# Talking-heads attention and two MoE layers on one core: scores of two pairs of heads as one piece of work, with four score banks and two pre-mix banks

## The chip, the cores and the metric

The kernel runs on one core of one Trainium2 chip. The metric is the time of one execution on the device in microseconds; lower is better.

## What is computed

The reference, cut to what matters (12 heads, 4 batches, 448 rows, head size 64, all float32):

```python
scores = 0.125 * q @ k.T                            # per batch b, head h: 448 x 448
scores = einsum('bhij,hg->bgij', scores, w_pre)     # pre-mix over heads
attn = softmax(scores, axis=-1)
attn = einsum('bhij,hg->bgij', attn, w_post)        # post-mix over heads
x = (attn @ v) as 1792 tokens x 768
h = x @ w_in; x = (h * cos(h)) @ w_out              # 768 -> 2048 -> 768
logits = x @ phi                                    # soft MoE, 8 experts x 4 slots
slots = softmax(logits, axis=0).T @ x               # per expert: relu(slots @ w1[e]) @ w2[e]
out = softmax(logits, axis=1) @ slot_outputs
```

## The kernel before, in words

The kernel has three phases: attention (phase_a, to about 513 us of the profiled span), the first layer with the logits (phase_b) and the soft MoE (phase_c). Only phase_a is touched.

phase_a works through 16 tiles (line 216): four batches, each cut into three tiles of 120 query rows and one of 90. For each tile and each of six pairs of heads there is a score (lines 346 to 389). `mul` (353) multiplies q by k for the two heads of a pair. q and k are each split into a high and a low part, so there are three products; the two heads lie on the two halves of the partitions (64 rows each), and their matmuls stand in two row halves of the array, each head in a PSUM bank of its own. That makes six matmuls. `out` (361) copies each head's bank to SBUF on ScalarE or VectorE, into one of eight places (`ssrc`), and `sort` (372) issues a transfer on the SP or POOL queue that puts the head's rows into the tile's `s2` in the order that the pre-mix wants. `s2` has two places, one per tile.

A tile has four groups of 30 rows (three in the smallest tile), 60 groups in all. `pre` (394) does three pieces for each group: one pre-mix matmul by a 120 x 120 matrix over the whole array into a "pre" bank, then the maximum on VectorE (408) and the exponential on ScalarE (412); the bank is free after the exponential. It needs all twelve sorted heads of its tile. `fin` (422) makes the post-mix weights, `post` (436) does four pieces for each group, each of three products into a "post" bank that is copied out (448), and `av` (485) multiplies a tile's mixed attention by v in three pieces with matmuls of 64 columns (half the array), each into one bank of the kind "ps". `k_prep` (286) and `q_prep` (309) transpose k and q into "ps" banks, from where ScalarE and VectorE split them. Beside all that, `narrow` (505) converts the next phase's weights from 64 to 32 bits on ScalarE, VectorE and GpSimd.

PSUM has eight banks. Three are for the pre-mix ("pre"), two for the post-mix ("post"), three for scores, transposes and av ("ps"); `PLACES` (24) says so. For the first 24 pieces that ask for "ps", `SPARE` (26) takes banks of all three kinds in turn, since the others are not yet used.

The order of the work is not written out by hand: a planner (`Plan`, lines 72 to 176) makes it before the kernel is built. Every piece of work is an `op` with the engines that may do it and a price on each, the pieces that it depends on, the places that it takes or uses, and a due time in units of groups. `schedule` (114) goes forward in time: for each engine it looks at the pieces that can start within 0.05 us of the earliest (145), and takes the one that is due first. A piece can start when its engine is free, its inputs are done, and all the places that it takes are free (`room`, 96). TensorE's pieces that use half the array (scores and av, `half=True`) and those that use all of it have a price of `TURN` = 0.095 us for going from one to the other (134), and a piece that would change the mode counts as due `STAY` = 0.4 groups later (146). Each engine then runs its instructions in the planned order; the semaphores, not the plan's times, set when they start.

A score of pair p in a tile whose first group is g0 is due at g0 - 3.2 - 3.6 (5 - p) / 5 (568). `qk[ti, p]` is its matmul piece; the next tile's `q_prep` and the next batch's `k_prep` wait for it before they write over q and k (303, 338), and some loads are put behind it (566, 573).

Of the kernel before, what the change touches and what calls it, by code (L numbers as in the profile page):

```python
# [9 lines left out]
F32 = mybir.dt.float32  # L10
# [10 lines left out]
AHEAD_AT = [v for v in range(16, 48) if v % 2 == 0] + 2 * [48, 49, 50, 51] + [52, 55, 56, 58, 60, 61]  # L21
LATER = {4: [0], 8: [1], 11: [2], 13: [3], 14: [4]}

PLACES = {"pre": 3, "post": 2, "ps": 3, "knat": 2, "qnat": 2, "ssrc": 8, "s2": 2, "e": 3, "wc": 2, "xst": 1,
          "raw": 4, "nar": 5, "cv_t": 2, "cv_m": 2}
SPARE = 3 * ["ps", "pre", "ps", "pre", "ps", "post", "pre", "post"]

K_DUE, S_DUE, S_SPAN, P_DUE, AV_DUE, AV_SPAN, STAY = 4.0, 3.2, 3.6, 1.8, 0.7, 3.0, 0.4

# [149 lines left out]
def phase_a(tc, ident, q, k, v, w_pre, w_post, xT_d, wide, start_next):  # L179
    nc = tc.nc  # L180
    B, H, S, D = q.shape
# [6 lines left out]
    with ExitStack() as ctx:  # L188
        early = ctx.enter_context(ExitStack())

        sg = early.enter_context(tc.tile_pool(name="a_groups", bufs=1))
        sp = early.enter_context(tc.tile_pool(name="a_sb", bufs=1))
        sn = early.enter_context(tc.tile_pool(name="a_nar", bufs=1))
        sl = ctx.enter_context(tc.tile_pool(name="a_late", bufs=1, side="right"))
        pp = ctx.enter_context(tc.tile_pool(name="a_pre", bufs=PLACES["pre"], space=PSUM))
        pq = ctx.enter_context(tc.tile_pool(name="a_post", bufs=PLACES["post"], space=PSUM))
        ps = ctx.enter_context(tc.tile_pool(name="a_ps", bufs=PLACES["ps"], space=PSUM))

# [4 lines left out]
        def room(pool, tag, shape, dtype, name):  # L203
            return pool.tile(shape, dtype, tag=tag, name=name, bufs=PLACES[tag])

        kp = sp.tile([128, H // 2, S], F32R, name="k_hi")
        kr = sp.tile([128, H // 2, S], F32R, name="k_lo")
        vt = sl.tile([CJ, H, NJ, D], F32, name="v")  # L210
        qh = sp.tile([128, H // 2, 120], F32R, name="q_hi")
        ql = sp.tile([128, H // 2, 120], F32R, name="q_lo")
        am = [sl.tile([CJ, H, NJ, 120], F32, name=f"am{i}") for i in range(2)]
# [6 lines left out]
        QUEUE = {"SP": nc.sync, "ACT": nc.scalar, "POOL": nc.gpsimd}  # L220
        PSUMS = {"ps": ps, "pre": pp, "post": pq}
        plan = Plan(PLACES, SPARE)

        def copy(by, out, in_):
            if by == "DVE":
                nc.vector.tensor_copy(out=out, in_=in_)
            else:
                nc.scalar.copy(out=out, in_=in_)  # L228

        def bank(slot, name):  # L230
            return PSUMS[slot.tag_used].tile([128, 512], F32, tag=slot.tag_used, name=name)

        made = {}
# [5 lines left out]
        kload, qload, vload, knat, qnat = {}, {}, {}, {}, {}  # L239
# [16 lines left out]
        def load_q(ti, part, due, behind):  # L256
            b, t = tiles[ti]
            m = H // 3
            if part == 0:
                qslot[ti] = Slot("qnat")  # L260

            def start():
                if part == 0:
                    qnat[ti] = room(sp, "qnat", [120, H, D], F32, f"qnat{ti}")
                h = m * part
                for r, n, i in ((0, 80, 360), (80, 10, S - 10)) if t == 3 else ((0, 120, 120 * t),):
                    nc.sync.dma_start(
                        out=qnat[ti][r:r + n, h:h + m],
                        in_=q[b, h:h + m, i:i + n, :].rearrange("h i d -> i h d"))
            qload[ti, part] = dma(1.0 if t == 3 else 0.5, 0.65, start, due=due, late=3.0 if ti > 1 else 0.0, takes=[qslot[ti]] if part == 0 else [],  # L270
                                  uses=[] if part == 0 else [qslot[ti]],
                                  behind=behind + ([qload[ti, 0]] if part else []))

        def load_v(b, c, due, behind):
            def start():
                nc.sync.dma_start(
                    out=vt[:, 4 * c:4 * c + 4],
                    in_=v[b, 4 * c:4 * c + 4].rearrange("h (p t) d -> p h t d", t=NJ))
            vload[b, c] = dma(0.55, 1.9, start, due=due, late=5.0,
                              deps=[avs[4 * b - 1, c]] if b else [], behind=behind)  # L280


        kdone, qdone, qk, sdone, avs, amdone = {}, {}, {}, {}, {}, {}
        EV = [("ACT", 0.44), ("DVE", 0.56)]
# [58 lines left out]

        s2l, s2t, sorted_ = {}, {}, {}

        def scores(ti, p, due):

            b, t = tiles[ti]
            n = ROWS[t]
            s = [Slot("ps") for _ in range(2)]  # L350
            x = {}

            def mul(e):
                pts = made["s", ti, p] = [bank(s[o], f"s{ti}_{2 * p + o}") for o in range(2)]
                for i, (x, y) in enumerate(((qh, kp), (qh, kr), (ql, kp))):
                    for o in range(2):
                        r = slice(64 * o, 64 * o + 64)
                        nc.tensor.matmul(pts[o][:n, :S], x[r, p, :n], y[r, p, :],  # L358
                                         start=(i == 0), stop=(i == 2))

            def out(o):
                def f(e):
                    if ti:
                        x[o] = room(sg, "ssrc", [120, S], F32, f"ss{ti}_{2 * p + o}")
                    else:

                        c = S * (2 * p + o)
                        x[o] = am[1].rearrange("p h t i -> p (h t i)")[:, c:c + S]
                    copy(e, x[o][:n], made["s", ti, p][o][:n, :S])
                return f  # L370

            def sort(o):
                h = 2 * p + o

                def f(e):
                    if h == 0:
                        s2t[ti] = room(sg, "s2", [120, 12, S], F32, f"s2_{ti}")
                    QUEUE[e].dma_start(out=s2t[ti][h::12, :n // 10], in_=x[o][:n])  # L378
                return f
            qk[ti, p] = plan.op([("PE", 0.8)], mul, [kdone[b, p], qdone[ti, p // 2]], due, takes=s, half=True)  # L380
            for o in range(2):
                h = 2 * p + o
                ss = [Slot("ssrc")] if ti else []
                if h == 0:
                    s2l[ti] = Slot("s2")
                c = plan.op(EV, out(o), [qk[ti, p]], due, takes=ss, uses=[s[o]])
                sorted_[ti, h] = plan.op([("SP", 1.0), ("POOL", 0.8)], sort(o), [c], due,
                                         takes=[] if h else [s2l[ti]], uses=ss + ([s2l[ti]] if h else []),
                                         moves=1.0 * n / 120, behind=[sorted_[ti, 0]] if h else [])

# [3 lines left out]
        def pre(gi, c, due):  # L394
# [5 lines left out]
            def mul(e):  # L400
                if c == 0:
                    et[gi] = sl.tile([120, 3, S], F32, tag="e", name=f"e{gi}", bufs=PLACES["e"])
                    mz[gi] = sl.tile([120, 3, 3], F32, tag="mz", name=f"mz{gi}", bufs=PLACES["e"])
# [51 lines left out]
        xst, xl = {}, {}  # L455
# [107 lines left out]
        for b in range(B):  # L563
            for ti in range(4 * b, 4 * b + 4):
                g0, n = first[ti], NG[tiles[ti][1]]
                mark = [qk[ti - 1, 0]] if ti > 2 else [qk[1, 5]] if ti > 1 else [qk[0, 2]] if ti else []
                for p in range(6):
                    d = g0 - S_DUE - S_SPAN * (5 - p) / 5
                    if p % 2 == 0:
                        load_q(ti, p // 2, d - K_DUE - 2 if ti == 0 else d - 2.1, mark)  # L570
                    if ti % 4 == 0:
                        for t in range(NJ) if p % 3 == 0 else ():
                            load_k(b, p // 3, t, d - K_DUE - 2, [qk[4 * b - 2, 0]] if b else [])
                        k_prep(b, p, d - K_DUE)
                    if p % 2 == 0:
                        q_prep(ti, p // 2, d - 0.3)
                    scores(ti, p, d)
                for gi in range(g0, g0 + n):
                    for c in range(3):
                        pre(gi, c, gi - P_DUE + c / 3)  # L580
                    f = fin(gi, gi - 0.4)
                    for jt in range(NJ):
                        post(gi, jt, f, gi + jt / 4)
                if ti % 4 == 0:
                    for c in range(3):
                        load_v(b, c, g0 + 2, [] if b else [mixed[2]])
                if ti < NT - 1:
                    av(ti, g0 + n + AV_DUE)
        for u in range(len(units)):
            due = N_FIRST + (N_LAST - N_FIRST) * u / (len(units) - 1)  # L590
# [632 lines left out]
```

## Time and profile before

| | |
|---|---|
| median of 3 runs | 947.32 us (946.84 to 953.72) |
| the profiled execution | 947.2 us, its span 945.4 us |
| TensorE busy in the span | 901.4 us, 95% |
| VectorE, ScalarE, GpSimd busy | 70%, 60%, 21% |
| mean granted TensorE clock | 0.988 |

All stretches and single times below are in microseconds from the start of that span. The time is a little longer than the span, since it also has what lies around the first and last instruction. PE is TensorE, PEld its weight loads, DVE VectorE, ACT ScalarE, POOL GpSimd, SP the engine that issues most transfers; L358 is line 358 of the kernel. Matmuls are pipelined and their ends are modelled, so neighbouring PE rows overlap; the step from one start to the next tells what a piece takes. [...]

### The profile page before, as it was taken

What the parts mean: (1) busy time and instruction counts of PE and PEld (TensorE: products, weight loads), DVE (VectorE), ACT (ScalarE), POOL (GpSimd) and SP (SyncE); (2) the same over time, 40 slices, a digit from 0 to 9 for tenths busy, and PEclk for the clock granted to TensorE, in tenths of its full rate; (3) what the DMA queues carried; (4) which work ended last, traced back from release to release, by engine and by line L of the source; (5) the groups of instructions that cost most, each with busy time, mean ns of one, the idle gap of its engine ahead of it and who ended that gap; (6) DMA issues with size and microseconds to landing.
All of it is one profiled execution on the core that took longest, in us unless ns stands there. A gap on an engine that the chain in (4) does not pass through costs nothing.

```text
span 945.4 us, 18209 instructions
## 1 busy us (share of the span) xinstructions
PE 901.4 (95%) x6720; PEld 648.5 (69%) x6720; DVE 663.4 (70%) x1294; ACT 563.6 (60%) x1241; POOL 196.5 (21%) x242
## 2 busy tenths in 40 slices
PE   7889999999999999999999999999999999989985
PEld 4556767776777777676778877777777787945522
DVE  4658998988989889898844755666766667833303
ACT  4556786777777777777654654565657558610102
POOL 2032444524544336453400000000000000000000
PEclk9989999999999999999999999999999999999897
DMA  7999778898788978988338731364464339899999
GB/s 161 209 183 210 202 208 212 187 245 233 210 224 205 252 197 200 226 222 237 109 95 248 218 114 51 112 211 132 147 215 136 106 114 299 276 355 379 373 373 330
DMA packets 195460, 198.92 MB, mean 210 GB/s; under 512 B 70916, under 2 KB 164752, under 8 KB 195372
## 3 DMA queue, kind: packets, MB, share of 16 engines
q1 hardware_dynamic: 185176, 176.97, 64.3%
q0 software_dynamic: 7584, 20.14, 8.9%
q8 instruction: 53, 0.87, 0.4%
q10 hardware_dynamic: 2612, 0.65, 0.3%
q14 instruction: 35, 0.29, 0.1%
HBM read 135.40 MB, written 23.59 MB: 168 GB/s over the span
## 4 chain that ended last, share of the span: by engine, by line
PE 73%; DVE 12%; DMA 7%; ACT 3%; issue 3%; SPq 1%; DVEq 0%; ACTq 0%
PE po L443 11%; PE pre L405 10%; PE h L710 8%; PE h L711 8%; PE h L713 8%; PE av L467 5%; PE s L358 5%; PE gt L750 3%; DMA early<-in_moe_w_dram 3%; PE eh L1030 2%; DMA s<-ss 2%; DVE cvt L531 2%; DVE mz L408 2%; PE etr L1039 2%; PE lg L759 2%
## 5 line engine op out<-in xcount | busy, mean ns | idle before, releaser
L443 PEld LDWEIGHTS po<-wc,e 120*112 120x112 f32 x1440 | 171.8, 177 | 63.8 <-issue 41.7
L443 PE MATMUL po<-wc,e 120*112 120x120 f32 x1440 | 184.7, 270 | 2.3 <-ACT am L228 1.0
L405 PE MATMUL pre<-s,kron_pre 120*120 120x448 f32 x360 | 166.5, 550 | 5.2 <-ACT e L412 2.7
L710 PE MATMUL h<-x,wh 128*128 128x512 f32 (+1 forms) x384 | 142.0, 380 | 0.0
L412 ACT ACTIVATE e<-pre,mz 120x448 f32<-120x448 f32 x180 | 114.8, 638 | 44.0 <-DVE mz L408 41.4
L711 PE MATMUL h<-x,wh 128*128 128x512 f32 (+1 forms) x384 | 136.2, 364 | 0.0
L408 DVE TENSOR_REDUCE mz<-pre 120x1 f32<-120x448 f32 x180 | 110.4, 618 | 27.9 <-PE pre L405 26.8
L228 ACT COPY am<-po 112x360 f32<-112x360 f32 x184 | 84.6, 464 | 50.7 <-PE po L443 49.2
L726 ACT ACTIVATE cg<-h,consts 128x512 f32<-128x512 f32 (+1 forms) x64 | 40.4, 632 | 89.0 <-PE h L713 86.5
L378 POOL DMA_DIRECT2D s<-ss x93 | 56.4, 607 | 178.6 <-ACT ss L228 106.4
L710 PEld LDWEIGHTS h<-x,wh 128*128 128x128 f32 x384 | 72.2, 188 | 23.0 <-ACT cg L726 8.0
L713 PE MATMUL h<-x,wf 128*128 128x512 f32 (+1 forms) x384 | 87.5, 363 | 0.0
L544 POOL TENSOR_TENSOR nar<-nar,cvm 128x384 f32<-128x384 f32 x64 | 65.0, 1015 | 86.1 <-DVE cvm L540 34.3
L467 PE MATMUL av<-am,v 112*64 112x120 f32 (+1 forms) x1536 | 82.5, 262 | 0.0
L467 PEld LDWEIGHTS av<-am,v 112*64 112x64 f32 x1536 | 74.0, 137 | 10.0 <-issue 5.1
L727 DVE TENSOR_SCALAR cg<-cg 128x512 f32<-128x512 f32 (+1 forms) x64 | 25.1, 392 | 78.9 <-ACT cg L726 78.5
L711 PEld LDWEIGHTS h<-x,wh 128*128 128x128 f32 x384 | 72.3, 188 | 10.6
L1036 POOL MEMSET hz<- 128x256 f32 x2 | 0.6, 304 | 358.5 <-DVE rz L985 358.5
L713 PEld LDWEIGHTS h<-x,wf 128*128 128x128 f32 x384 | 66.3, 188 | 11.9
L228 ACT COPY ss<-s 120x448 f32<-120x448 f32 (+1 forms) x111 | 56.9, 532 | 25.1 <-PE s L358 14.4
L547 POOL TENSOR_TENSOR nar<-nar,cvt 128x384 f32<-128x384 f32 x64 | 68.5, 1070 | 4.0
L655 DVE TENSOR_TENSOR wf<-wf,wh 128x768 fp32r<-128x768 f32 x64 | 60.9, 952 | 9.9 <-ACT wh L654 9.9
(183 smaller groups left out, 1474.9 us busy)
## 6 DMA issues: line engine op xcount, KB each, us to landing
early<-in_moe_w_dram SPq DMA_DIRECT2D x36, 768.0 KB
wf<-w SPq DMA_DIRECT2D x64, 384.0 KB
s<-ss POOLq DMA_DIRECT2D x74, 210.0 KB, 6.3
s<-ss SPq DMA_DIRECT2D x70, 210.0 KB
raw<-in_moe_w_in_dram SPq DMA_DIRECT2D x32, 384.0 KB
w<-nar SPq DMA_DIRECT2D x64, 192.0 KB
raw<-in_moe_w_out_dram SPq DMA_DIRECT2D x32, 384.0 KB
gn<-in_moe_w_dram SPq DMA_DIRECT2D x16, 768.0 KB
```

The source lines that it names most:

```text
L228: nc.scalar.copy(out=out, in_=in_)
L405: nc.tensor.matmul(prt[gi, c][:, :S], kpre, s2t[ti][:, 3 * g + c, :], start=True, stop=True)
L408: nc.vector.tensor_reduce(out=mz[gi][:, 0, c:c + 1], in_=prt[gi, c][:, :S], axis=AX.X, op=ALU.max, negate=True)
L412: nc.scalar.activation(out=et[gi][:, c, :], in_=prt.pop((gi, c))[:, :S], func=AF.Exp, bias=mz[gi][:, 0, c:c + 1], accum_out=mz[gi][:, 1, c ...
L443: nc.tensor.matmul(pt[:, :360].rearrange("p (g i) -> p g i", i=30)[:, :, 10 * c:10 * c + 10], et[gi][:, c, jt * CJ:(jt + 1) * CJ], wct[gi] ...
L467: nc.tensor.matmul(pt[64 * o:64 * o + 64, x * 120:x * 120 + n], vt[:, g, jt, :], am[ti % 2][:, g, jt, :n], start=(jt == 0), stop=(jt == NJ ...
L544: nc.gpsimd.tensor_tensor(out=x["f"], in0=x["f"], in1=x["m"], op=ALU.mult)
L547: nc.gpsimd.tensor_tensor(out=x["f"], in0=x["f"], in1=x["t"].bitcast(F32), op=ALU.add)
L655: nc.vector.tensor_tensor(out=wf_t[v], in0=wf_t[v].bitcast(F32), in1=wh.bitcast(F32), op=ALU.subtract)
L710: nc.tensor.matmul(pt, wh[:, c], xh[:, c, :], start=(c == 0), stop=False)
L711: nc.tensor.matmul(pt, wh[:, c], xl[:, c, :], start=False, stop=False)
L713: nc.tensor.matmul(pt, wl[:, c], xh[:, c, :], start=False, stop=(c == 5))
```

## The change

From the third tile on (`ti >= 2`), `scores` is called once for two pairs of heads instead of once for each. The piece has twelve matmuls, pair after pair, takes four "ps" banks at once, and is due 0.36 groups before the second pair's old due time, which is midway between the two. Its price in the plan is 0.1 + 0.6 for each pair (0.7 for one, 1.3 for two; it was 0.8 for one). The copies and sorts stay one for each head, and wait for the whole piece. "ps" gets four banks and "pre" two, and the order in `SPARE` is adapted.

```diff
--- before.py
+++ after.py
@@ -21,9 +21,9 @@
 AHEAD_AT = [v for v in range(16, 48) if v % 2 == 0] + 2 * [48, 49, 50, 51] + [52, 55, 56, 58, 60, 61]
 LATER = {4: [0], 8: [1], 11: [2], 13: [3], 14: [4]}
 
-PLACES = {"pre": 3, "post": 2, "ps": 3, "knat": 2, "qnat": 2, "ssrc": 8, "s2": 2, "e": 3, "wc": 2, "xst": 1,
+PLACES = {"pre": 2, "post": 2, "ps": 4, "knat": 2, "qnat": 2, "ssrc": 8, "s2": 2, "e": 3, "wc": 2, "xst": 1,
           "raw": 4, "nar": 5, "cv_t": 2, "cv_m": 2}
-SPARE = 3 * ["ps", "pre", "ps", "pre", "ps", "post", "pre", "post"]
+SPARE = 3 * ["ps", "pre", "ps", "post", "ps", "pre", "ps", "post"]
 
 K_DUE, S_DUE, S_SPAN, P_DUE, AV_DUE, AV_SPAN, STAY = 4.0, 3.2, 3.6, 1.8, 0.7, 3.0, 0.4
 
@@ -343,48 +343,51 @@
 
         s2l, s2t, sorted_ = {}, {}, {}
 
-        def scores(ti, p, due):
+        def scores(ti, pairs, due):
+
 
             b, t = tiles[ti]
             n = ROWS[t]
-            s = [Slot("ps") for _ in range(2)]
+            s = {h: Slot("ps") for p in pairs for h in (2 * p, 2 * p + 1)}
             x = {}
 
             def mul(e):
-                pts = made["s", ti, p] = [bank(s[o], f"s{ti}_{2 * p + o}") for o in range(2)]
-                for i, (x, y) in enumerate(((qh, kp), (qh, kr), (ql, kp))):
-                    for o in range(2):
-                        r = slice(64 * o, 64 * o + 64)
-                        nc.tensor.matmul(pts[o][:n, :S], x[r, p, :n], y[r, p, :],
-                                         start=(i == 0), stop=(i == 2))
-
-            def out(o):
+                for h in s:
+                    made["s", ti, h] = bank(s[h], f"s{ti}_{h}")
+                for p in pairs:
+                    for i, (a, c) in enumerate(((qh, kp), (qh, kr), (ql, kp))):
+                        for o in range(2):
+                            r = slice(64 * o, 64 * o + 64)
+                            nc.tensor.matmul(made["s", ti, 2 * p + o][:n, :S], a[r, p, :n], c[r, p, :],
+                                             start=(i == 0), stop=(i == 2))
+
+            def out(h):
                 def f(e):
                     if ti:
-                        x[o] = room(sg, "ssrc", [120, S], F32, f"ss{ti}_{2 * p + o}")
+                        x[h] = room(sg, "ssrc", [120, S], F32, f"ss{ti}_{h}")
                     else:
 
-                        c = S * (2 * p + o)
-                        x[o] = am[1].rearrange("p h t i -> p (h t i)")[:, c:c + S]
-                    copy(e, x[o][:n], made["s", ti, p][o][:n, :S])
+                        x[h] = am[1].rearrange("p h t i -> p (h t i)")[:, S * h:S * h + S]
+                    copy(e, x[h][:n], made["s", ti, h][:n, :S])
                 return f
 
-            def sort(o):
-                h = 2 * p + o
-
+            def sort(h):
                 def f(e):
                     if h == 0:
                         s2t[ti] = room(sg, "s2", [120, 12, S], F32, f"s2_{ti}")
-                    QUEUE[e].dma_start(out=s2t[ti][h::12, :n // 10], in_=x[o][:n])
+                    QUEUE[e].dma_start(out=s2t[ti][h::12, :n // 10], in_=x[h][:n])
                 return f
-            qk[ti, p] = plan.op([("PE", 0.8)], mul, [kdone[b, p], qdone[ti, p // 2]], due, takes=s, half=True)
-            for o in range(2):
-                h = 2 * p + o
+            m = plan.op([("PE", 0.1 + 0.6 * len(pairs))], mul,
+                        [kdone[b, p] for p in pairs] + [qdone[ti, p // 2] for p in pairs], due,
+                        takes=list(s.values()), half=True)
+            for p in pairs:
+                qk[ti, p] = m
+            for h in s:
                 ss = [Slot("ssrc")] if ti else []
                 if h == 0:
                     s2l[ti] = Slot("s2")
-                c = plan.op(EV, out(o), [qk[ti, p]], due, takes=ss, uses=[s[o]])
-                sorted_[ti, h] = plan.op([("SP", 1.0), ("POOL", 0.8)], sort(o), [c], due,
+                c = plan.op(EV, out(h), [m], due, takes=ss, uses=[s[h]])
+                sorted_[ti, h] = plan.op([("SP", 1.0), ("POOL", 0.8)], sort(h), [c], due,
                                          takes=[] if h else [s2l[ti]], uses=ss + ([s2l[ti]] if h else []),
                                          moves=1.0 * n / 120, behind=[sorted_[ti, 0]] if h else [])
 
@@ -574,7 +577,10 @@
                         k_prep(b, p, d - K_DUE)
                     if p % 2 == 0:
                         q_prep(ti, p // 2, d - 0.3)
-                    scores(ti, p, d)
+                    if ti < 2:
+                        scores(ti, [p], d)
+                    elif p % 2:
+                        scores(ti, [p - 1, p], d - S_SPAN / 10)
                 for gi in range(g0, g0 + n):
                     for c in range(3):
                         pre(gi, c, gi - P_DUE + c / 3)
```

## Rows read from the trace of the kernel before

**Rows 1.** The page: the chain that ended last, its largest shares by line.
```profile
PE 901.4 (95%) x6720; PEld 648.5 (69%) x6720; DVE 663.4 (70%) x1294; ACT 563.6 (60%) x1241; POOL 196.5 (21%) x242
...
PE po L443 11%; PE pre L405 10%; PE h L710 8%; PE h L711 8%; PE h L713 8%; PE av L467 5%; PE s L358 5%; PE gt L750 3%; DMA early<-in_moe_w_dram 3%; PE eh L1030 2%; DMA s<-ss 2%; DVE cvt L531 2%; DVE mz L408 2%; PE etr L1039 2%; PE lg L759 2%
```

**Rows 2.** Stretches: length; busy PE, PEld, DVE, ACT, POOL (instructions); clock, DMA share, GB/s.
```profile
61.00:68.00 7.00, 4.22 (x14) 3.02 (x15) 1.33 (x2) 3.48 (x9) 2.78 (x3) 0.55 0.79 159
...
100.00:450.00 350.00, 342.58 (x2911) 249.55 (x2912) 317.79 (x628) 257.37 (x661) 158.32 (x181) 1.00 0.84 216
...
500.00:520.00 20.00, 20.00 (x259) 18.09 (x258) 7.34 (x14) 9.23 (x19) 0.00 (x0) 1.00 0.79 239
```

**Rows 3.** TensorE in order of time, 316 to 320 us: start, length, line, operation, tiles.
```profile
316.26 0.46 PE L358 MATMUL s<-k_hi,q_hi 64*120 64x448 f32 x2
316.56 0.37 PE L358 MATMUL s<-k_lo,q_hi 64*120 64x448 f32 x2
316.77 0.37 PE L358 MATMUL s<-k_hi,q_lo 64*120 64x448 f32 x2
317.06 0.87 PE L443 MATMUL po<-wc,e 120*112 120x120 f32 x6
317.77 0.92 PE L405 MATMUL pre<-s,kron_pre 120*120 120x448 f32 x2
318.52 0.78 PE L443 MATMUL po<-wc,e 120*112 120x120 f32 x6
319.14 0.92 PE L405 MATMUL pre<-s,kron_pre 120*120 120x448 f32 x2
```

**Rows 4.** TensorE in order of time, the first tile's scores back to back.
```profile
10.57 0.58 PE L358 MATMUL s<-k_lo,q_hi 64*90 64x448 f32 x2
10.94 0.58 PE L358 MATMUL s<-k_hi,q_lo 64*90 64x448 f32 x2
11.31 0.58 PE L358 MATMUL s<-k_hi,q_hi 64*90 64x448 f32 x2
```

**Rows 5.** TensorE in order of time: the third tile's first score, and the last score.
```profile
46.21 0.47 PE L358 MATMUL s<-k_hi,q_hi 64*120 64x448 f32 x2
...
472.73 0.78 PE L443 MATMUL po<-wc,e 120*112 120x120 f32 x6
473.44 1.86 PE L467 MATMUL av<-am,v 112*64 112x120 f32 x32
475.23 0.44 PE L358 MATMUL s<-k_hi,q_hi 64*90 64x448 f32 x2
```

**Rows 6.** Pre-mixes (PE) and exponentials (ACT) two places earlier, in order of time.
```profile
89.30 1.01 PE L405 MATMUL pre<-s,kron_pre 120*120 120x448 f32 x2 [1.80 <-ACT e L412]
89.58 0.63 ACT L412 ACTIVATE e<-pre,mz 120x448 f32<-120x448 f32 x1 [0.34 <-DVE mz L408]
...
467.48 0.64 ACT L412 ACTIVATE e<-pre,mz 120x448 f32<-120x448 f32 x1
467.67 0.92 PE L405 MATMUL pre<-s,kron_pre 120*120 120x448 f32 x2
```

**Rows 7.** Groups by line: busy, mean ns | idle before them <-releasers.
```profile
L443 PE MATMUL po<-wc,e 120*112 120x120 f32 x1440 | 184.7, 270 | 2.3 <-ACT am L228 1.0 <-DVE am L226 0.8 <-DVE wc L430 0.6
...
L358 PE MATMUL s<-k_hi,q_hi 64*120 64x448 f32 (+1 forms) x192 | 47.6, 461 | 7.5 <-ACT ss L228 4.9 <-DVE ss L226 1.2 <-ACT q_hi L228 0.7
```

**Rows 8.** All engines in order of time, the wait near 60 us; [idle before <-releaser].
```profile
63.20 0.97 ACT L228 COPY ss<-s 120x448 f32<-120x448 f32 x2 [4.81 <-DMA s<-ss]
...
63.78 1.16 PE L358 MATMUL s<-k_hi,q_hi 64*120 64x448 f32 x2 [4.30 <-ACT ss L228]
...
68.44 0.82 PE L443 MATMUL po<-wc,e 120*112 120x120 f32 x6
```

**Rows 9.** In order of time: the tenth tile's last copies, its first pre-mix.
```profile
292.31 0.97 ACT L228 COPY ss<-s 120x448 f32<-120x448 f32 x2 [0.17 <-PE s L358]
...
300.87 0.92 PE L405 MATMUL pre<-s,kron_pre 120*120 120x448 f32 x2
```

## The prediction

> **What bounds the kernel now.** I read the page first: TensorE is busy for 95% of the span, and the chain that ended last is mostly TensorE too, with the post-mix (po), the pre-mix (pre) and the scores (s) of the attention phase among its largest parts [rows 1]. Next come the stretches. From 100 to 450 us TensorE has 342.6 of 350 us, VectorE 317.8 (91%), ScalarE 257.4 (74%); from 500 to 520 us, where the attention phase hands over to the next, TensorE is full [rows 2]. So a TensorE time saved between 64 and 500 us comes off the end, as long as VectorE and ScalarE keep pace. Up to 64 us TensorE also waits for transfers (the wait in [rows 8] is the last long one), and I count no saving before it.
>
> Then the order of TensorE's instructions. A busy TensorE is not read from the lengths of its rows, which overlap, but from one start to the next. In [rows 3] a post-mix between whole-array pieces takes 318.52 to 319.14, 0.62 us. The one behind a score takes 317.06 to 317.77, 0.71. The score itself takes 316.26 to 317.06, 0.80: 0.30 to its second step, 0.21 to the third, 0.29 to the next piece. So a lone score of one pair costs 0.80 us and about 0.10 on each neighbour that uses the whole array; I call each 0.10 a turn.
>
> **The change, part by part.**
>
> *Two pairs in one piece.* Twelve matmuls run where six did, with one beginning and one end. What is the seam in the middle worth? The first tile has scores back to back: 10.57, 10.94, 11.31 [rows 4]. The inner step has 0.37, and the step over the seam into the next pair (10.94 to 11.31) again 0.37. A seam costs no more than an inner step; only the first and the last step bear a surcharge. With the steps of [rows 3] a double score takes 0.30 + 4 x 0.20 + 0.30 = 1.40 us against 2 x 0.80, so 0.20 saved. From the third tile on there are 14 tiles x 3 doubles = 42. I take off the three of the third tile, which lies before 64 us: 39 x 0.20 = 7.8 us. The bounds: nothing, if the seam costs an end and a beginning, and 7.8; I take 7.8, because the row of the seam shows no surcharge.
>
> *Turns.* By themselves, 42 pieces fewer would also save 84 turns. But the av product (L467) works in halves of the array too and now often stands right beside a score: the post-mix before the av at 473.44 takes 472.73 to 473.44, 0.71, then av 1.79 (to 475.23), then the score [rows 5]. In the timeline from the score at 46.21 to the one at 475.23 I counted 84 scores and 37 runs of av; they make 75 unbroken stretches of half-array work, of which 41 are a lone score and 34 of the av runs touch a score. Each stretch costs two turns. After the change a double takes all four score banks, and an av needs one of the same banks. An av directly ahead holds a bank that the double waits for, and an av directly behind waits until one of the double's banks is copied out. The planner takes what can start within 0.05 us of the first, so other work goes between. I count 42 + 37 = 79 stretches: 4 more, 8 turns, 0.8 us lost. Bounds: 84 stretches, if no two avs touch (9 more, 1.8 us lost), to 45, if all 34 avs find a double (30 fewer, 6.0 us gained). I take 0.8.
>
> *Two banks for the pre-mix.* A bank is held from the matmul until ScalarE's exponential has ended. The pre-mix at 89.30 began when the exponential of the one two places earlier began only at 89.58 and took 0.63; likewise the last such, 467.67 against an exponential that ran from 467.48 for 0.64 [rows 6]. From 64 us on there are 18 of these among some 160, late by 13.7 us in all; with about 0.2 us from end to start each, 17 us is the upper bound. The lower is zero, since the planner knows of two banks and puts a post-mix or a score in that place. The nearest row is the post-mix, which has two banks already: 240 pieces of work, and TensorE idles 2.3 us ahead of them [rows 7]. I take 2.5.
>
> *Four banks for scores.* A double waits until all four are free, and afterwards four copies of about 0.53 (ScalarE) or 0.62 us come at once where two came. The exponentials and maxima queue behind them. Scores idle TensorE for 7.5 us now [rows 7], of which 4.3 is one place at 63.78 [rows 8]; so 3.2 over 95 others. Pre- and post-mix fill the time while banks drain; without that cover each of 39 doubles would wait some 0.55 us for the copy of an av ahead of it (0.20 plus 0.35), 21 us. I take 1.0 more than now. Below zero it goes only if the one place vanishes, which is a rival.
>
> *The rest.* Number and shape of copies, sort transfers and their engines stay. The scores' due time is the mean of the two old ones, so the sort of a tile is on average as early as before; its four transfers come in a bunch on the SP and POOL queues. The new order of banks for the first 24 pieces spreads them over the same eight banks; I give it nothing. The price in the plan (0.7 for a single, 1.3 for a double, against 0.8 each) only moves the order.
>
> The sum: -7.8 + 0.8 + 2.5 + 1.0 = -3.5. The profiled execution took 947.2 us, 0.1 under the median of the runs, so 947.2 - 3.5 = **943.7 us**.
>
> **The rivals.**
>
> *The copies are the next bound.* VectorE at 91% is close behind TensorE [rows 2], and the doubles bunch its work. Then the 7.8 us turn into waits for copies, and only the losses stay: between 947.2 and 947.2 + 4.3 = 951.5; I say 949. For it: VectorE's share. Against it: ScalarE has 93 us free in those 350 and shares the copies. The Trainium skill speaks for this rival: in "TensorEngine Tiling (Array Packing)", section "PSUM Bottleneck", it says that tiling speeds up TensorE but not the evacuation of PSUM, so that the copy may become the bottleneck. By that rule the time would be this rival's; the trace bears it out only so far as VectorE's 91%.
>
> *Slower: the sort of each tile comes late.* A tile's pre-mix needs all its twelve heads sorted. In the tenth tile the last two copies run from 292.31 to 293.28, and its first pre-mix is at 300.87 [rows 9], 7.6 us later: there is little spare. If the last double of a tile first waits for an av's bank (1.79 + 0.55 = 2.3 us) and then has two copies more to wait for (0.6 with two engines), the pre-mixes come 2.9 us later. If TensorE finds other work for half of that, 1.45 us is lost in each of 13 tiles: 18.9 us, and 943.7 + 18.9 = 962.6. From 0.27 us a tile it is slower than before. Against it: TensorE had enough to do in every such gap until now, and the double's due time is earlier than that of its second pair was.
>
> *Faster: the stall at 59.5 to 68.4 us goes.* There ScalarE's copy of a score waits 4.81 us for a sort transfer, and TensorE's next score waits 4.30 us for its bank [rows 8]. From 61 to 68 us the granted clock is 0.55, so nearly all of it was spent at the lower level, 1.2 GHz [rows 2]. The score, post-mix and pre-mix behind the wait take 63.78 to 68.44, 4.66 us, instead of 0.80 + 0.71 + 0.75 = 2.26, so 4.30 + 2.40 = 6.7 us are at stake. If the double finds its four banks free ahead of the late transfer and the work behind it fills the wait, 937.0. Against it: the copies still need a landed sort, and block ScalarE for all else.
>
> *Faster: the avs stay beside the doubles.* Then the turns are -6.0 instead of +0.8: 936.9. Only if the banks come free just in time.
>
> **How the numbers follow.** Chances: forecast 0.48 (its own range 939.5 to 948), copies the next bound 0.18, late sorts 0.14, stall gone 0.11, avs beside doubles 0.09. A measurement of this kernel can tell about 1% from no change, so the limits are 937.8 and 956.8. The two faster rivals lie just under the lower one: of their 0.20 I count 0.16 as faster by over 1%. Of the late sorts' 0.14 nearly all, 0.13, is slower by over 1%. The rest, 0.71, is within. The range reaches from 935.5, below the two faster cases, to 955, which leaves out the late sorts.
>
> **What would show it.** A double score from its first start to the next piece takes 1.40 us (1.60 if the seam is dear); some 79 half-array stretches; no av directly beside a double; TensorE's idle ahead of pre-mixes up by 2 to 3 us, ahead of scores by about one; the last post-mix of the attention phase some 3.5 us earlier. If the pre-mixes of each tile begin later after the last copy than 7 to 9 us, and TensorE idles there, the slower rival is right. If TensorE's busy time falls but the phase ends where it did, with waits on VectorE, the copies were the bound. A time under 938 or over 955 would prove the forecast wrong.

## The result, and the profile after

The changed kernel is slower: median 956.06 us (949.37 to 961.75, 18 runs) against 947.70 us (943.95 to 954.10, 18 runs) for the kernel before. The ratio is 1.008, with a 95% interval of 1.0064 to 1.0096, so by the ratio 7.6 us are lost where 3.5 us were forecast to be won. The profiled execution took 961.75 us, the slowest of the 18, so prices below come from the ratios, and the rows of profiles show places.

The page's engines and chain of the changed kernel (L446 is the post-mix, L408 the pre-mix, L361 the score, L470 av), beside [rows 1]:

```profile
PE 901.0 (94%) x6720; PEld 653.7 (68%) x6720; DVE 660.7 (69%) x1300; ACT 562.3 (59%) x1235; POOL 201.2 (21%) x249
...
PE po L446 9%; PE pre L408 9%; PE h L716 8%; PE h L717 8%; PE h L719 8%; PE av L470 5%; PE s L361 4%; DMA s<-ss 4%; PE gt L756 3%; DMA early<-in_moe_w_dram 3%; DVE mz L411 2%; PE eh L1036 2%; SPq L249 2%; DVE cvt L534 2%; PE lg L765 1%
```

TensorE is as busy as before in a longer span. In the chain the scores' share fell from 5% to 4%, and that of the sorts (s<-ss) rose from 2% to 4%. The stretches, beside [rows 2]:

```profile
61.00:68.00 7.00, 3.52 (x12) 2.66 (x13) 3.58 (x8) 2.17 (x7) 0.00 (x0) 0.50 0.94 231
100.00:450.00 350.00, 336.04 (x2842) 249.30 (x2841) 310.66 (x624) 251.71 (x642) 161.11 (x185) 0.99 0.85 209
500.00:520.00 20.00, 20.00 (x196) 16.38 (x195) 9.77 (x25) 10.83 (x31) 0.00 (x0) 1.00 0.58 183
```

From 100 to 450 us TensorE has 336.0 us of work where it had 342.6, and VectorE 310.7 (89%) where it had 317.8 (91%): neither engine has more to do, both wait more. What TensorE waits for stands in its groups, beside [rows 7]:

```profile
L408 PE MATMUL pre<-s,kron_pre 120*120 120x448 f32 x360 | 173.0, 568 | 22.1 <-ACT e L415 16.6 <-DMA s<-ss 3.8 <-DMA v<-in_v_dram 1.1
L446 PE MATMUL po<-wc,e 120*112 120x120 f32 x1440 | 183.9, 271 | 3.6 <-DVE am L226 3.6
L470 PE MATMUL av<-am,v 112*64 112x120 f32 (+1 forms) x1536 | 81.9, 262 | 2.5 <-ACT ss L228 1.8 <-DVE ss L226 0.6
L361 PE MATMUL s<-k_hi,q_hi 64*120 64x448 f32 (+1 forms) x192 | 42.1, 423 | 1.0 <-ACT q_hi L228 0.7 <-DVE q_lo L337 0.3
```

The idle ahead of pre-mixes rose from 5.2 to 22.1 us, most of it for an exponential, that is for a bank; ahead of scores it fell from 7.5 to 1.0. A single wait has 9.8 of the 22.1. It stands where [rows 8] had its wait of 4.30. From all engines in order of time (SPq is the SP queue):

```profile
49.24 5.43 SPq L249 DMA_DIRECT2D knat<-in_k_dram  x2
55.00 0.79 SPq L378 DMA_DIRECT2D s<-ss  x1
...
56.39 6.10 SPq L249 DMA_DIRECT2D knat<-in_k_dram  x4
...
62.52 0.62 DVE L226 COPY ss<-s 120x448 f32<-120x448 f32 x1 [11.51 <-DMA s<-ss]
...
63.71 0.63 ACT L415 ACTIVATE e<-pre,mz 120x448 f32<-120x448 f32 x1 [9.64 <-DVE mz L411]
...
64.48 1.85 PE L408 MATMUL pre<-s,kron_pre 120*120 120x448 f32 x2 [9.82 <-ACT e L415]
```

This is read from the bottom up: the pre-mix waits for a bank, the bank for an exponential, that for a maximum on VectorE, and VectorE stands for 11.5 us before the copy of a score, until a sort has landed. That sort left on the SP queue at 55.00 only, behind four loads of k that held the queue from 39.1 to 54.7 us, the last two of them in the first row. From 61 to 68 us the granted clock is 0.50, the lower level of 1.2 GHz.

A double score, TensorE in order of time:

```profile
49.44 0.47 PE L361 MATMUL s<-k_hi,q_hi 64*120 64x448 f32 x2
49.74 0.37 PE L361 MATMUL s<-k_lo,q_hi 64*120 64x448 f32 x2
49.95 0.36 PE L361 MATMUL s<-k_hi,q_lo 64*120 64x448 f32 x2
50.15 0.36 PE L361 MATMUL s<-k_hi,q_hi 64*120 64x448 f32 x2
50.35 0.37 PE L361 MATMUL s<-k_lo,q_hi 64*120 64x448 f32 x2
50.55 0.37 PE L361 MATMUL s<-k_hi,q_lo 64*120 64x448 f32 x2
50.85 0.87 PE L446 MATMUL po<-wc,e 120*112 120x120 f32 x6
```

From 49.44 to 50.85 it takes 1.41 us, with a seam (49.95 to 50.15) of 0.20. The piece takes what the forecast said; the loss lies elsewhere.

### The profile page after: what moved, and what is told of

Read it like the earlier page. It is cut to its first block, busy times and chain, and to the rows that moved or that the text cites. A ratio compares the mean times of both kernels' runs of the same rounds, so it can differ in the third digit from the quotient of the medians.

```text
span 960.0 us, 18259 instructions
## 1 busy us (share of the span) xinstructions
PE 901.0 (94%) x6720; PEld 653.7 (68%) x6720; DVE 660.7 (69%) x1300; ACT 562.3 (59%) x1235; POOL 201.2 (21%) x249
## 4 chain that ended last, share of the span: by engine, by line
PE 67%; DVE 14%; DMA 8%; issue 4%; ACT 4%; SPq 3%; POOL 1%; DVEq 0%; ACTq 0%; POOLq 0%
PE po L446 9%; PE pre L408 9%; PE h L716 8%; PE h L717 8%; PE h L719 8%; PE av L470 5%; PE s L361 4%; DMA s<-ss 4%; PE gt L756 3%; DMA early<-in_moe_w_dram 3%; DVE mz L411 2%; PE eh L1036 2%; SPq L249 2%; DVE cvt L534 2%; PE lg L765 1%
## 5 line engine op out<-in xcount | busy, mean ns | idle before, releaser
L446 PEld LDWEIGHTS po<-wc,e 120*112 120x112 f32 x1440 | 171.8, 179 | 63.8 <-issue 44.7
L408 PE MATMUL pre<-s,kron_pre 120*120 120x448 f32 x360 | 173.0, 568 | 22.1 <-ACT e L415 16.6
L446 PE MATMUL po<-wc,e 120*112 120x120 f32 x1440 | 183.9, 271 | 3.6 <-DVE am L226 3.6
L378 POOL DMA_DIRECT2D s<-ss x100 | 59.6, 598 | 126.4 <-ACT ss L228 90.0
L470 PE MATMUL av<-am,v 112*64 112x120 f32 (+1 forms) x1536 | 81.9, 262 | 2.5 <-ACT ss L228 1.8
L408 PEld LDWEIGHTS pre<-s,kron_pre 120*120 120x120 f32 x360 | 53.4, 186 | 44.6 <-ACT e L415 27.7
L470 PEld LDWEIGHTS av<-am,v 112*64 112x64 f32 x1536 | 74.0, 137 | 9.8 <-ACT ss L228 2.5
L719 PEld LDWEIGHTS h<-x,wf 128*128 128x128 f32 x384 | 66.3, 188 | 11.8
```

The lines of the kernel that those rows point to most:

```text
L408: nc.tensor.matmul(prt[gi, c][:, :S], kpre, s2t[ti][:, 3 * g + c, :], start=True, stop=True)
L446: nc.tensor.matmul(pt[:, :360].rearrange("p (g i) -> p g i", i=30)[:, :, 10 * c:10 * c + 10], et[gi][:, c, jt * CJ:(jt + 1) * CJ], wct[gi] ...
L470: nc.tensor.matmul(pt[64 * o:64 * o + 64, x * 120:x * 120 + n], vt[:, g, jt, :], am[ti % 2][:, g, jt, :n], start=(jt == 0), stop=(jt == NJ ...
L719: nc.tensor.matmul(pt, wl[:, c], xh[:, c, :], start=False, stop=(c == 5))
```

## The experiments

A double is a score of two pairs in one piece; "banks 4/2" means four banks for scores and two for the pre-mix. Theory A: the loss is the one wait near 60 us. Theory B: the lack of the third pre-mix bank costs in all tiles. Theory C: doubles themselves delay work. All ratios are to the kernel before, with 95% intervals from 6 to 18 runs of each changed kernel; 0.001 is 0.95 us. Waits and places are read from one profiled execution of each.

### The banks

**Doubles a tile later (e1)**, `if ti < 3:` in place of `if ti < 2:`.

> The changed kernel with doubles from the fourth tile on instead of the third; banks 4/2 stay. Theory A (the loss is one stall: the third tile's bunched copies wait for sort transfers that stand behind the second batch's loads of k, near 55 to 64 us): the wait of 9.8 us falls to 4 us or less, and about 5 to 8 us come back: a ratio to the kernel before near 1.000 to 1.002. Theory B (two banks for the pre-mix hold TensorE in all tiles): ratio stays near 1.006 to 1.009. Theory C (doubles drain the banks and delay each tile's sort): stays near 1.007.

1.0037 (1.0013 to 1.0062), between the ranges of theories A and B. The wait is 4.8 us in its profile, about what the kernel before has, and 0.0043 or 4.1 us came back; the 3.5 us that are left are not the wait.

**Banks 4/2 with single scores everywhere (e2)**, `if ti < NT:`.

> The changed kernel with single scores everywhere, so only the banks (four for scores, two for the pre-mix), their first order and the price 0.7 are changed. Theory A: near the kernel before, ratio 0.998 to 1.003, since single scores do not bunch the copies of the third tile. Theory B: slower by what the pre-mix waits cost, with no saving in the scores beside it: ratio 1.008 to 1.016, TensorE's idle ahead of pre-mixes above 12 us. Theory C: no loss, ratio 1.000.

1.0061 (1.0039 to 1.0083), above theory A's range and a little below theory B's; the idle ahead of pre-mixes is 11.8 us. The banks, with their new order and the lower price of a single score, bring most of the loss without any double. The wait is there as well, so it isn't the doubles' bunched copies that make it:

```profile
62.37 1.54 PE L446 MATMUL po<-wc,e 120*112 120x120 f32 x6 [10.27 <-ACT am L228]
```

And with four banks single scores stand back to back by themselves, 17 times between 64 and 500 us. TensorE in that kernel:

```profile
290.30 0.47 PE L361 MATMUL s<-k_hi,q_hi 64*120 64x448 f32 x2
...
290.81 0.37 PE L361 MATMUL s<-k_hi,q_lo 64*120 64x448 f32 x2
291.01 0.36 PE L361 MATMUL s<-k_hi,q_hi 64*120 64x448 f32 x2
...
291.71 0.87 PE L446 MATMUL po<-wc,e 120*112 120x120 f32 x6
```

Two single scores take 290.30 to 291.71, the same 1.41 us as a double. From the third tile's first score to the last score there are 62 unbroken half-array stretches, against 73 in the kernel before and 72 in the changed one.

**The kernel before with one pre-mix bank less (e3)**: `"pre": 2` for 3, one bank unused, `SPARE` without the third.

> The kernel before with two banks for the pre-mix and three for scores, one bank unused. Theory B: ratio 1.006 to 1.012, with idle ahead of pre-mixes of 10 us or more where it was 5. Theories A and C: ratio 0.998 to 1.003.

1.0056 (1.0031 to 1.0081), 5.3 us. The wait near 60 us is 3.3 us here, less than before, so the wait isn't in it: this is the price of the bank. Its group:

```profile
L405 PE MATMUL pre<-s,kron_pre 120*120 120x448 f32 x360 | 169.0, 557 | 10.2 <-ACT e L412 8.0 <-DMA s<-ss 1.1 <-DMA v<-in_v_dram 1.0
```

Theory B holds, with a ratio just under its range: the idle ahead of pre-mixes is 10.2 us, 5.0 more than the 5.2 of the kernel before, and most of it is for an exponential.

### The wait near 60 us

**The changed kernel with the third tile's sorts on POOL alone (e4)**:

```diff
-                sorted_[ti, h] = plan.op([("SP", 1.0), ("POOL", 0.8)], sort(h), [c], due,
+                sorted_[ti, h] = plan.op([("POOL", 0.8)] if ti == 2 else [("SP", 1.0), ("POOL", 0.8)], sort(h), [c], due,
```

> The changed kernel with the third tile's twelve sorts on the POOL queue alone, so that none stands on the SP queue behind the loads of k. Theory A: the wait near 64 us shrinks from 9.8 us to 3 to 6, ratio 1.002 to 1.005; if the transfers are late on any queue, as the wires are full, the wait stays at 8 or more. Theories B and C: ratio stays near 1.008.

1.0065 (1.0040 to 1.0089), above theory A's range and not clearly better than 1.0080. The wait is gone, though. The stretch from 25 to 64 us, first of the changed kernel, then of this one:

```profile
25.00:64.00 39.00, 27.01 (x156) 17.70 (x155) 18.77 (x40) 18.94 (x48) 5.81 (x10) 0.93 1.00 190
```

```profile
25.00:64.00 39.00, 37.51 (x247) 25.70 (x247) 28.55 (x59) 26.59 (x68) 11.94 (x19) 1.00 1.06 205
```

TensorE has 37.5 us of work there instead of 27.0. By the ratios only about 1.4 us of these 10.5 are kept, and that isn't clear. The two profiles can't show where the rest goes, as they are the fastest run of one kernel (951.45 us) and the slowest of the other; the largest later wait of this kernel is 4.65 us ahead of the eleventh tile's first pre-mix.

**The kernel before with the same edit (e12).**

> The kernel before with the third tile's sorts on the POOL queue alone, nothing else changed. Theory A: its own smaller stall (4.3 us of idle and 2.4 us at the lower clock near 60 us) goes, ratio 0.992 to 0.996. If the time is given back behind it, 0.998 to 1.001.

1.0004 (0.9979 to 1.0028): its own wait of 4.30 us is gone, and at 74.5 us it waits 3.9 us for loaded k instead. Theory A falls as the whole cause: in this kernel the wait's time is given back.

**Banks 4/2, single scores, the third tile's sorts on POOL (e15)**: beside the changed kernel with that edit only the doubles differ, and neither has the wait.

> Banks 4/2, single scores everywhere, the third tile's sorts on the POOL queue: beside the changed kernel with the same sorts (1.0065, e4) it differs in the doubles alone, and neither has the long wait near 60 us. If doubles save what their pieces show (22 more pairs joined at 0.2 us, less some 10 turns at 0.2), it is 2 to 3 us slower than that, ratio 1.008 to 1.010. If doubles cost more elsewhere than they save (theory C), it is faster: 1.000 to 1.004, which is then the price of the second pre-mix bank less what single scores save by standing together.

1.0025 (1.0006 to 1.0044), against 1.0065 (1.0040 to 1.0089) with doubles. So doubles don't save 2 to 3 us, but cost about 3.8; the intervals overlap at their ends. Against e2 (1.0061) the move of the sorts gave 3.4 us back.

### The doubles where no bank is short

**All eight banks in one ring (e5)**, for pre-mix, post-mix, scores, transposes and av alike, with single scores:

```diff
-PLACES = {"pre": 3, "post": 2, "ps": 3, ...
+PLACES = {"ps": 8, ...
-SPARE = 3 * ["ps", "pre", "ps", "pre", "ps", "post", "pre", "post"]
+SPARE = []
...
-            b = Slot("pre")
+            b = Slot("ps")
...
-            b = Slot("post")
+            b = Slot("ps")
```

> The kernel before with all eight banks in one ring that pre-mix, post-mix, scores, transposes and av take from in turn; scores stay single. No kind of work has a bank count of its own any more. If the loss of the change is the second pre-mix bank's waiting (theory B), the ring also takes away what little of it three banks leave: TensorE's idle ahead of pre-mixes falls from 5.2 us to 3 or less, and the time to a ratio of 0.990 to 0.999. If banks never were the point (theories A and C), ratio 0.998 to 1.002.

0.9948 (0.9924 to 0.9973), though it has the wait near 60 us as well (10.1 us). Outside that wait 2.4 us of idle are left ahead of its pre-mixes, as theory B expected.

**The same ring with doubles from the fourth tile on (e6).**

> The same ring of eight banks with doubles from the fourth tile on. Theory B: the doubles' saving of 39 x 0.2 us is no longer paid for with pre-mix banks, and the time is 4 to 8 us under the ring with singles, ratio to the kernel before 0.984 to 0.994. Theory C (doubles themselves delay the sorts and bunch the copies): no faster than the ring with singles, or slower.

1.0007 (0.9982 to 1.0033): clearly slower than the ring with single scores, and theory B doesn't explain this. But the pair is not pure. This kernel is made from the changed one and e5 from the one before, so the plan's price of a single score differs too (0.7 and 0.8), and TensorE's orders part near 46 us, where both kernels still have single scores only. The price differs in the two pairs on the ring below as well. In the profiles the loss stands early: the third tile's first pre-mix begins 7.1 us later than in e5 (93.1 against 86.0), and the attention phase ends 6.9 us later.

**Ring with doubles, but single scores in the first tile of each batch (e8)**, `if ti < 3 or ti % 4 == 0:`.

> The ring of eight banks with doubles from the fourth tile on, but single scores in the first tile of each batch, where a double has to wait for two newly turned pairs of k. Theory C, in this form: the doubles lose at the change of batches, and with singles there the ring with doubles comes to the ring with singles or below, ratio 0.990 to 0.996. If doubles lose in every tile alike, it stays near 1.000.

1.0066 (1.0040 to 1.0092), outside both ranges: fewer doubles, and 5.6 us slower than e6. A wait for newly turned k at the change of batches doesn't explain the loss. No run changes the order of the work and nothing else, so how many us of such a difference come from the order alone isn't known; this run warns that it may be several.

**Both rings with the third tile's sorts on POOL**, single scores (e9) first, then doubles (e11).

> The ring of eight banks with single scores, and the third tile's sorts on the POOL queue alone. Theory A: the stall of 10 us near 50 to 62 us, which the ring has too, shrinks as it did in the changed kernel with this edit, and 4 to 8 us come off: ratio 0.986 to 0.991. If later work gives it back, as it seemed to there, ratio 0.994 to 0.997.

0.9896 (0.9866 to 0.9926), 4.9 us under e5, with intervals that just touch. Here the time seems to stay won.

> The ring of eight banks, doubles from the fourth tile on, and the third tile's sorts on the POOL queue alone: beside the ring with single scores and the same sorts (0.990) it differs in the doubles alone, with no stall at the third tile in either. If the doubles' loss on the ring came from work that the stall piles up, it is gone here: ratio 0.984 to 0.990. If doubles cost more than they save wherever singles can stand together by themselves, 0.993 to 0.998.

0.9980 (0.9965 to 0.9995), 8 us slower than e9. By their pieces the doubles should have saved here: behind 64 us 38 pairs stand joined against 14, and half-array stretches are 46 against 59, since avs do stand beside doubles on the ring; at 0.2 us each that is 7.4 us. In the profiles the kernel with doubles is 4.6 us ahead at the sixth tile's first pre-mix and 10.7 us behind at the end of the phase; it loses 7.1 us from there to the seventh tile's and 5.7 us from the tenth's to the eleventh's. In that kernel, the eleventh tile's last four copies, their sorts, and the tile's first pre-mix:

```profile
313.56 1.23 DVE L224 COPY ss<-s 120x448 f32<-120x448 f32 x2 [0.37 <-PE s L359]
...
313.85 0.96 ACT L226 COPY ss<-s 120x448 f32<-120x448 f32 x2
...
314.67 1.18 POOL L376 DMA_DIRECT2D s<-ss  x2 [5.28 <-ACT ss L226]
...
320.37 3.08 SPq L515 DMA_DIRECT2D raw<-in_moe_w_out_dram  x1
...
323.55 1.65 SPq L376 DMA_DIRECT2D s<-ss  x2
...
337.29 1.07 PE L406 MATMUL pre<-s,kron_pre 120*120 120x448 f32 x1 [5.40 <-DMA qnat<-in_q_dram]
```

Four copies end together at 314.8; two sorts leave on POOL at once, two on the SP queue only at 323.55, behind loads that take that queue up to 3 us each. TensorE then stands 5.4 us, and 4.5 us at the seventh tile. The row names a load of q, which the pre-mix doesn't read: the load has its semaphore in common with the sort of 323.55, and the pre-mix needs that sort, so the wait is put down to the sort by inference. Those are the tiles during which the next batch's k is loaded. The time in us from a tile's last copy to its first pre-mix, from the traces, for four tiles in which it grew with doubles:

| tile | before | 4/2 single (e2) | changed | ring single (e9) | ring doubles (e11) |
|---|---|---|---|---|---|
| 7th | 15.0 | 17.0 | 18.7 | 15.8 | 21.2 |
| 9th | 6.9 | 10.1 | 13.2 | 7.3 | 13.3 |
| 11th | 15.4 | 19.5 | 22.1 | 18.1 | 22.5 |
| 13th | 9.9 | 9.9 | 10.7 | 7.3 | 13.6 |

These tiles are chosen. Over the fourth to the sixteenth tile the gaps add up to 163.6 us with doubles on the ring and 144.2 with single scores, but with banks 4/2 to 161.4 in the changed kernel and 165.7 in e2.

**All sorts on POOL**, doubles (e13) first, then single scores (e14).

> The ring of eight banks, doubles from the fourth tile on, and all sorts of all tiles on the POOL queue. Theory D: a double's four sorts come in a bunch, two of them stand on the SP queue behind loads, and at the seventh and eleventh tile, where the next batch's k is loaded, the pre-mix then waits for them. With no sort on the SP queue the time from last copy to first pre-mix falls there from 21 and 22 us to 17 or less, the waits of 4.5 and 5.4 us go, and the ratio falls from 0.998 to 0.985 to 0.991. If the doubles lose in another way it stays at 0.995 or more.

> The ring of eight banks, single scores, and all sorts on the POOL queue: the control for the run before. Theory D: single scores lose little on the SP queue, so little changes, ratio 0.986 to 0.992, against 0.990 with the third tile's sorts alone moved. If sorts on POOL slow the weight conversion or delay each other, 0.993 or more.

0.9993 (0.9975 to 1.0012) and 0.9995 (0.9972 to 1.0019), both above what theory D, as the first expectation states it, had asked for. With no sort on the SP queue the doubles' gap at the seventh and eleventh tile is that of the single scores (15.3 and 18.5 against 16.8 and 18.0), and the waits of 4.5 and 5.4 us are gone. But neither kernel gained: a POOL queue with all the sorts costs single scores 1%, so the control moved. In the profiled executions the doubles' attention phase ended 7.6 us later (510.6 against 503.0 us). Of that, 6.2 us are there at the first tile's first pre-mix, far ahead of any double, first in e13, then in e14:

```profile
37.97 2.57 PE L406 MATMUL pre<-s,kron_pre 120*120 120x448 f32 x3 [12.09 <-DMA s<-ss]
```

```profile
31.82 1.82 PE L403 MATMUL pre<-s,kron_pre 120*120 120x448 f32 x2 [6.27 <-issue]
```

VectorE's and ScalarE's orders part near 18.5 us, in the copies of the first tile's single scores, where the two kernels differ only in the plan's price of a single score. Behind that place the doubles lose 1.4 us more, and the single-score kernel lost 6.2 us in one wait right after the phase. So with the sorts off the SP queue the two waits are gone, and in this pair little else speaks against doubles; but no saving shows either, and that the sorts are all that doubles cost elsewhere is not shown.

### VectorE behind its plan

**Doubles from the fourth tile on, banks 4/2, with corrected prices (e7)**:

```diff
-            t = plan.op([("DVE", 0.42)], bits, [ld], due, takes=[ts], uses=[raws])
-            t = plan.op([("DVE", 0.62)], sign, [t], due, uses=[raws, ts])
-            t = plan.op([("DVE", 0.58)], least, [t, m], due, uses=[ts, ms])
+            t = plan.op([("DVE", 0.47)], bits, [ld], due, takes=[ts], uses=[raws])
+            t = plan.op([("DVE", 0.83)], sign, [t], due, uses=[raws, ts])
+            t = plan.op([("DVE", 0.73)], least, [t, m], due, uses=[ts, ms])
```

> Doubles from the fourth tile on with banks 4/2, and the plan's prices of three VectorE steps of the weight conversion raised to what the trace shows (0.42 to 0.47, 0.62 to 0.83, 0.58 to 0.73). If two pre-mix banks cost so much because VectorE runs behind its plan and the maxima come late, the idle ahead of pre-mixes falls from 12.9 us to 6 or less and the ratio from 1.004 to 0.998 to 1.001. If the wait is set by the banks and not by the plan's error, it stays at 1.003 to 1.005.

1.0015 (1.0002 to 1.0028), with 9.2 us of idle ahead of pre-mixes instead of 12.9: between the two ranges, and its interval overlaps that of 1.0037. So that VectorE's lateness is part of the bank's price is likely, but not shown.

**The ring with single scores and these prices (e10)**, and the same with the third tile's sorts on POOL (e16).

> The ring of eight banks with single scores and the three prices of the weight conversion raised as before. With no kind of work short of banks the plan's error should matter less: ratio 0.991 to 0.996, against 0.995 for the ring alone; if VectorE's lateness is the bound there too, 0.990 or less.

0.9939 (0.9911 to 0.9966): no difference that can be told from 0.9948.

> The ring of eight banks with single scores, the third tile's sorts on POOL (0.990) and the three corrected prices of the conversion. If VectorE's lateness against its plan still costs TensorE time there, 0.983 to 0.987; if the ring has taken up that slack, 0.988 to 0.992.

0.9834 (0.9801 to 0.9868), a median of 933.70 us: 1.7% faster than the kernel before, and the best of all. That is 5.9 us under e9, with intervals that just touch, where the same prices gave nothing in e10; as a new price is also a new order, the cause stays open. In its group of pre-mixes 3.0 us of idle are left, and none of them for an exponential:

```profile
L403 PE MATMUL pre<-s,kron_pre 120*120 120x448 f32 x360 | 163.8, 548 | 3.0 <-DMA qnat<-in_q_dram 1.0 <-ACT ss L226 1.0 <-DMA s<-am 1.0
```

## Why the prediction was wrong, step by step

- *A double takes 1.40 us*: right, 1.41.
- *Turns, 79 stretches, 0.8 us lost*: the rule was right for these banks, no av stands beside a double; but avs joined each other more often, and 72 stretches remain. The 75 that I counted in the kernel before are 73 by its trace, so there is one stretch less and 0.2 us won. A small miss.
- *Two pre-mix banks, 2.5 us*: the first step that failed. The measured price is 5.3 us (interval 2.9 to 7.7). I took the nearest row, the post-mix with two banks and 2.3 us of idle, but its bank is held only for one copy. From the matmul's start to the end of its last reader that is 1.4 us at the median in the kernel before; a pre-mix bank, which goes through VectorE and then ScalarE, is held 2.9 us.
- *7.8 us of saved pieces come off the end*: the second, and the larger one. I compared a double with two lone scores. With four banks the planner puts single scores together anyway (17 times in e2), so 39 doubles join 22 pairs more, 22 x 0.2 = 4.4 us, and there are 72 - 62 = 10 stretches more, 10 x 0.2 = 2.0 us lost. Even those 2.4 us didn't show. Three pairs differ in the doubles alone. The doubles came out 1.8 us slower in the changed kernel than in e2 (1.0080 against 1.0061, not clear), 3.8 us slower in e4 than in e15, and 2.3 us faster in e1 than in e2 (not clear), where the wait near 60 us is 5.5 us shorter. On the ring they were 5.6 and 8 us slower, with the price of a single score changed beside them, and no slower with all sorts on POOL.
- *Four score banks, 1.0 us*: the scores' own idle fell from 7.5 to 1.0 us. What bunching was seen to cost is the sort, for which I had put nothing but a rival.
- *Nothing before 64 us*: I counted no saving there, and no loss. In the profile the wait grew by 5.5 us. I had it as a rival for the faster side only. What it is worth isn't one number: 4.1 us came back in e1, about 1.4 in e4 (not clear), 3.4 in e15, none in the kernel before, 4.9 on the ring.

Of the rivals, the late sorts are the nearest. Their mechanism was seen, with gaps 1 to 6 us longer in the four tiles of the table, but not in all thirteen; 962.6 was too much. The copies as the bound (949) were not it: from 100 to 450 us VectorE's share fell from 91% to 89%. The Trainium skill's rule on PSUM evacuation ("TensorEngine Tiling (Array Packing)", "PSUM Bottleneck"), that the copy may become the bottleneck, is not borne out here: what was short was not copying capacity but banks, each held until VectorE and ScalarE were through.

Together, in ratios: banks 4/2 with single scores cost 5.8 us (the lost pre-mix bank 5.3, the longer wait, less what joined scores give), doubles on top 1.8. Put the other way, the bank cost 2.8 us more than forecast, and all the rest cost 2.3 us where it was forecast to gain 6.0. How the longer wait and the doubles share those 8.3 us stays open, as does what part of the doubles' loss on the ring is theirs and not the order's.

## What to carry to other kernels

A saving in a piece of work is to be compared with what the planner does without it under the same new resources, not with the piece as it stands today: here the banks alone joined 17 of the 39 pairs. Price a bank by how long it is held, not by another kind of work with the same count; and where kinds of work compete for banks, try one ring for all beside a split. Transfers that come in a bunch land as late as the last of them, and a queue that also carries loads sets when that is. And where a planner makes the order, a control has to keep every price in it: here a price 0.1 us lower went with a first pre-mix 6 us later.

## What the runs showed of the hardware that I had not expected

Two steps of the weight conversion on VectorE, with two SBUF inputs each, take twice as long when GpSimd works beside them. In the changed kernel, GpSimd, VectorE and ScalarE in order of time:

```profile
254.68 1.04 POOL L547 TENSOR_TENSOR nar<-nar,cvm 128x384 f32<-128x384 f32 x1 [2.16 <-DVE cvm L543]
...
254.89 1.24 DVE L534 SCALAR_TENSOR_TENSOR cvt<-raw,cvt 128x384 uint32<-128x384 uint32 x1
...
256.37 0.65 DVE L431 TENSOR_SCALAR mz<-mz 120x3 f32<-120x3 f32 x1
...
257.72 0.62 DVE L411 TENSOR_REDUCE mz<-pre 120x1 f32<-120x448 f32 x1
...
258.37 0.63 ACT L415 ACTIVATE e<-pre,mz 120x448 f32<-120x448 f32 x1 [1.71 <-DVE mz L411]
```

The step at 254.89, which takes 0.55 us by itself, starts while GpSimd multiplies and takes 1.24. All 31 such steps that overlap a multiplication or addition on GpSimd began while it ran; 28 of them took over 0.8 us (mean 1.11), and of the 33 others none (mean 0.55). The second such step (L539) has 1.19 and 0.55. The maximum, whose one input is in PSUM, has 0.62 either way. A step with one SBUF input isn't always spared: the one at 256.37 takes 0.65 beside GpSimd and 0.16 alone. The plan had 0.62 for the first step, so VectorE is behind its plan here, and the next exponential waits 1.71 us for its maximum. The Trainium skill states the rule for two inputs in "SBUF — State Buffer", section "Who interferes with whom": a VectorE instruction with two SBUF inputs contends with a GpSimd instruction that reads SBUF. The trace agrees, with 1.11 us against 0.55.
